# Sharing out small steps of attention and mixing, an early table load, and a new order of the whole program

## The chip, the cores and the metric

The program runs on one core of a Trainium2 chip. The time is device microseconds from one launch, and the value compared is the median of several runs. All work of the core is in one program: TensorE (PE) multiplies, VectorE (DVE), ScalarE (ACT) and GpSimd (POOL) do everything elementwise, and SyncE (SP) issues the DMAs.

## The reference

Attention with a mask by blocks of 64 positions, then a mixer over the joined heads. The inputs q, k, v are 8 batches x 8 heads x 576 positions x 64; the mixer's weights are 512 x 512, 576 x 576 (two) and 512 x 512. All is float32.

```python
scores = q @ k.transpose(0, 1, 3, 2) / sqrt(D)
scores = where(pos[:, None] // 64 >= pos[None, :] // 64, scores, -1e9)
attn = exp(scores - scores.max(-1)); attn = attn / (attn.sum(-1) + 1e-9)
x = (attn @ v), heads joined: [8, 576, 512]
theta = x @ w_theta
zr, zi = x * cos(theta), x * sin(theta)
y = einsum('ts,bsd->btd', w_tok_r, zr) + einsum('ts,bsd->btd', w_tok_i, zi)
u = x + y
out = u + maximum(u @ w_ch, 0)
```

## The kernel before

The eight batches go through two phases that overlap: while batch b is mixed, the attention of batch b + 1 is computed. Heads are taken in pairs (p from 0 to 31, four to a batch; head n = 2p + hh). For accuracy most products are made of two halves: a float32 operand is split into a high and a low part, and three products stand for one. The first twelve pairs use plain float32 scores, the first four pairs plain float32 weights of attention, turned by TensorE.

The program is a list of 2757 parts. A part is a small function with a key; it issues one or a few instructions, nearly always on one engine. PLACES gives each part its place, the list is sorted by it, and the instructions are issued in that order, so that the order in which each engine takes its work is written out by hand. BANKS gives the PSUM bank to each group of products in the order of their starts; a group waits until the former user of its bank has been read. ON gives, letter by letter, the engine of those parts that more than one engine can do (D VectorE, A ScalarE, P GpSimd). RUNNING lists filling products: at a place, so many products of the constant `ones` into a bank that nobody needs (L1113). Waits between engines follow from the data.

The parts that matter here, with the lines that stand in the profile:

- `sab`, `sc`, `sd` (L600, L605, L612): the scores of a pair in three groups. `m` (L638, L630) on VectorE takes the maxima out of PSUM, `e` (L642) on ScalarE the exponentials.
- `tp`, `cp` (L654, L661, L663): for the first four pairs, transposes by TensorE and their copies out of PSUM. For the others `high` and `low` (L327 or L331, L669) split the exponentials into `p`, and a transposing DMA makes `pt`.
- `vz`, `vr`, `vb`, `vm` (L505, L509, L353, L359): the size of a batch's v: two sums over pieces on ScalarE, one addition on VectorE, a diagonal on GpSimd, one product on TensorE. The scale of v follows, then the scaled v (`vf`, or `v1` and `v2`, L586).
- `weighted` (L689): the weighted sums of one head, with the sum of the weights in an extra column.
- `normalise`, steps 0 to 3 (L697 or L699, L701, L706, L709): a small number is added, the reciprocal taken, four or five tiles of 64 columns are multiplied by it out of PSUM into `x_ring` in one instruction on VectorE (step 2), and for the second head of a pair a block of 64 rows more (step 3).
- `again` (L715): a block of 64 rows by 64 columns of `x_ring` is copied to the other 64 partitions, twice for a pair, on GpSimd.
- The mixer: `xh`, `xl` split x (L325 or L331, L775); `theta` (L789) multiplies; `turns` and `rest` (L799, L805) reduce the angle, `size` (L811) takes its absolute value; `sines`, steps 0 to 2 (L823, L825), take cosine and sine, step 0 and 1 of two wide tiles each, step 2 of the last, narrow one; `z`, `zh`, `zl` (L835, L325 to L331, L848) multiply by x and split; `mix` (L858) multiplies by the token weights, `u` (L871) collects; `c` (L891) multiplies by the channel weights, `out` (L897) and `fin` finish, and a DMA stores.

Sine and exponential are not in one table of ScalarE: the build puts a table load ahead of the first activation that needs the other one (ACT_TABLE_LOAD; it carries the line of that activation and stands behind the activation's wait).

Of the kernel before, what the change touches and what calls it, by code (L numbers as in the profile page):

```python
# [32 lines left out]
    3, 2, 15, 19, 21, 62, 162, 197, 4, 5, 22, 30, 34, 65, 177, 191, 27, 26, 52, 61, 64, 92, 246, 255, 43, 40, 74,  # L33
    78, 91, 113, 217, 221, 73, 69, 103, 106, 112, 118, 212, 236, 99, 96, 131, 136, 139, 172, 239, 244, 116, 145,
    154, 165, 167, 219, 227, 146, 182, 226, 234, 242, 252, 429, 578, 178, 174, 198, 229, 249, 256, 361, 449, 82,
    85, 107, 111, 121, 135, 143, 151, 183, 187, 193, 196, 204, 206, 207, 356, 268, 271, 301, 310, 330, 348, 358,
    375, 185, 195, 275, 343, 383, 411, 392, 415, 419, 0, 1, 11, 7, 33, 10, 39, 35, 70, 12, 86, 101, 9, 45, 48, 50,
    53, 55, 57, 60, 63, 284, 499, 287, 130, 179, 77, 152, 324, 81, 125, 345, 328, 157, 370, 377, 173, 192, 233,
    247, 250, 253, 267, 274, 290, 523, 951, 684, 423, 521, 366, 565, 546, 347, 553, 609, 612, 492, 630, 705, 547,
    575, 596, 605, 618, 623, 640, 645, 647, 788, 1284, 903, 686, 528, 716, 771, 790, 712, 844, 899, 894, 753, 993,  # L40
    982, 843, 855, 875, 878, 882, 886, 896, 902, 948, 1073, 1600, 1131, 1022, 1017, 1090, 1104, 1093, 1036, 1192,
    1220, 1205, 1117, 1319, 1306, 1143, 1164, 1208, 1212, 1221, 1226, 1237, 1239, 1245, 1255, 1434, 1574, 1371,
    1367, 1362, 1478, 1443, 1424, 1460, 1564, 1561, 1439, 1671, 1676, 1472, 1507, 1513, 1516, 1532, 1547, 1549,
    1559, 1590, 1680, 2121, 1878, 1739, 1704, 1760, 1835, 1735, 1766, 1846, 1926, 1842, 1742, 1974, 1948, 1818,
    1852, 1868, 1904, 1937, 1947, 1950, 1961, 1964, 1984, 2227, 2165, 2071, 2016, 1997, 2130, 2099, 2102, 2139,
    2234, 2229, 2120, 2329, 2324, 2118, 2156, 2164, 2167, 2204, 2207, 2236, 2270, 2273, 2517, 2546, 2549, 6, 67, 8,
    16, 13, 14, 18, 25, 29, 17, 28, 24, 31, 32, 36, 47, 38, 51, 20, 44, 49, 41, 46, 72, 94, 108, 120, 37, 42, 54,
    59, 93, 117, 119, 124, 266, 122, 126, 23, 76, 58, 66, 56, 68, 75, 84, 88, 80, 79, 87, 83, 104, 98, 97, 102,
    100, 90, 89, 95, 105, 110, 129, 153, 158, 160, 123, 134, 109, 115, 147, 181, 186, 189, 273, 188, 272, 71, 132,
    292, 114, 138, 142, 128, 133, 144, 150, 156, 137, 141, 140, 149, 155, 161, 164, 163, 159, 175, 184, 180, 190,  # L50
    201, 216, 224, 225, 171, 176, 166, 170, 214, 230, 240, 254, 258, 248, 295, 127, 168, 289, 194, 199, 169, 200,
    208, 205, 203, 202, 220, 215, 223, 218, 209, 211, 213, 222, 210, 228, 232, 231, 237, 241, 261, 269, 276, 235,
    245, 238, 243, 264, 283, 285, 291, 298, 288, 300, 148, 303, 362, 251, 282, 302, 259, 270, 297, 294, 320, 277,
    279, 281, 286, 306, 316, 307, 326, 325, 311, 322, 318, 332, 368, 379, 381, 382, 329, 344, 339, 351, 385, 399,
    401, 418, 438, 413, 431, 262, 319, 335, 359, 364, 374, 365, 388, 373, 372, 387, 396, 402, 409, 406, 389, 391,
    390, 400, 404, 417, 427, 426, 433, 476, 488, 489, 490, 425, 443, 442, 450, 498, 513, 514, 535, 539, 522, 534,
# [176 lines left out]
def attention_phase_mixer(  # L233
# [10 lines left out]
    nc = tc.nc  # L244
# [922 lines left out]
```

## Time and profile before

| | |
|---|---|
| median of 3 runs | 663.51 us (662.39 to 667.03) |
| profiled execution, own time | 661.59 us |
| span from first to last instruction | 659.8 us |
| TensorE products, busy | 643.2 us (97%) |
| VectorE, ScalarE, GpSimd busy | 580.5, 466.7, 328.2 us |
| granted clock of TensorE, mean | 0.997 |

The profiled execution is one of many and has its own time; its span is what the profiler saw between the first and the last instruction. A busy TensorE is not one at its peak: products overlap, and their ends are modelled.

### The profile page before, as it was taken

The numbers are of one execution on the slowest core, as the hardware profiler recorded it, in microseconds if no ns is written. First come the engines' busy times: TensorE is split into PE (matmuls) and PEld (weight loads), VectorE is DVE, ScalarE is ACT, GpSimd is POOL, SyncE is SP. The second block draws the span as 40 slices with busy tenths as digits, with TensorE's granted clock in tenths as the row PEclk, the third lists the DMA queues.
The fourth block names the chain that finished last, engine by engine and source line by source line (L and its number), as shares of the span: only waits on it lengthen the run. The fifth ranks groups of instructions, "written<-read, shape, count | busy, mean of one in ns | idle before, by whom it ended". The sixth has DMA issues, their size and how long they took to land.

```text
span 659.8 us, 17344 instructions
## 1 busy us (share of the span) xinstructions
PE 643.2 (97%) x7153; PEld 504.0 (76%) x7153; DVE 580.5 (88%) x900; ACT 466.7 (71%) x719; POOL 328.2 (50%) x345
## 2 busy tenths in 40 slices
PE   8999989999999999999999999999999999999997
PEld 4899767887678767787787868887787867885775
DVE  4899999989999999999998998999879999754724
ACT  4997897775997788665984679678885887516411
POOL 2310357545528737585256466554574346552800
PEclk9999989999999999999999999999999999999999
DMA  8972288999999799699687879899678887740021
GB/s 308 352 254 77 47 205 145 201 221 180 229 199 182 175 190 192 144 202 177 158 201 187 150 177 183 185 210 240 120 175 160 139 192 131 113 114 19 1 90 73
DMA packets 247647, 110.51 MB, mean 167 GB/s; under 512 B 229008, under 2 KB 229008, under 8 KB 247568
## 3 DMA queue, kind: packets, MB, share of 16 engines
q1 hardware_dynamic: 247568, 109.41, 75.3%
q8 instruction: 56, 0.92, 0.6%
q14 instruction: 23, 0.19, 0.1%
HBM read 43.06 MB, written 9.44 MB: 80 GB/s over the span
## 4 chain that ended last, share of the span: by engine, by line
PE 68%; DVE 21%; ACT 5%; issue 4%; DMA 1%; POOL 0%; DVEq 0%; ACTq 0%; POOLq 0%
PE ps L858 25%; PE ps L891 10%; PE ps L689 10%; PE ps L789 10%; PE ps L600 9%; DVE m L638 5%; DVE p L669 3%; DVE v L586 2%; ACT t L642 1%; ACT p L327 1%; PE ps L654 1%; DVE zl L848 1%; PE ps L1113 1%; DVE u L897 1%; DVE wT_l L436 1%
## 5 line engine op out<-in xcount | busy, mean ns | idle before, releaser
L642 ACT ACTIVATE t<-ps,m 128x192 f32<-128x192 f32 (+4 forms) x288 | 140.8, 555 | 58.8 <-DVE m L638 40.2
L858 PE MATMUL ps<-wT_h,zl 128*128 128x288 f16 x540 | 155.0, 287 | 2.5 <-DVE zl L848 2.5
L858 PE MATMUL ps<-wT_h,zh 128*128 128x288 f16 x540 | 155.4, 288 | 0.7 <-ACT t L642 0.7
L858 PE MATMUL ps<-wT_l,zh 128*128 128x288 f16 x540 | 154.9, 287 | 0.0
L638 DVE TENSOR_REDUCE m<-ps 128x2 f32<-128x640 f32 (+3 forms) x128 | 117.4, 946 | 12.0 <-PE ps L605 11.5
L858 PEld LDWEIGHTS <-zh 128*128 128x128 f16 x1080 | 106.1, 98 | 27.8 <-issue 1.1
L689 PE MATMUL ps<-v,pt 128*128 128x65 f16 (+2 forms) x2668 | 113.3, 201 | 3.8 <-DVE x_ring L706 2.5
L669 DVE SCALAR_TENSOR_TENSOR p<-t,p 128x1664 f16<-128x1664 f32 x56 | 111.8, 2002 | 2.6 <-ACT p L327 2.5
L891 PE MATMUL ps<-uhl,wch_h 128*128 128x288 f16 x512 | 95.4, 286 | 1.1 <-DVE u L897 1.0
L689 PEld LDWEIGHTS <-pt 128*128 128x128 f16 x2436 | 81.5, 97 | 8.8 <-issue 5.5
L789 PE MATMUL ps<-wth_h,xt 128*128 128x512 f16 (+1 forms) x384 | 87.3, 345 | 0.3 <-DVE u L871 0.3
L789 PEld LDWEIGHTS <-xt 128*128 128x128 f16 (+1 forms) x576 | 46.4, 102 | 43.7 <-issue 2.4
L327 ACT ACTIVATE p<-t 128x1664 f16<-128x1664 f32 x46 | 73.3, 1599 | 3.7 <-DMA pt<-p 3.4
L891 PE MATMUL ps<-uhl,wch_l 128*128 128x288 f16 x256 | 73.2, 286 | 0.0
L858 PEld LDWEIGHTS <-zl 128*128 128x128 f16 x540 | 53.1, 98 | 16.3 <-DVE zl L848 3.2
L715 POOL COPY x_ring<-x_ring 64x64 f32<-64x64 f32 x64 | 37.9, 592 | 49.8 <-DVE x_ring L709 22.0
L891 PEld LDWEIGHTS <-wch_h 128*128 128x128 f16 x512 | 48.6, 98 | 14.8 <-issue 2.2
L789 PE MATMUL ps<-wth_l,xt 128*128 128x512 f16 (+1 forms) x192 | 57.3, 344 | 0.0
L835 POOL TENSOR_TENSOR aa<-aa,x_ring 128x512 f32<-128x512 f32 (+1 forms) x27 | 34.1, 1265 | 43.0 <-ACT aa L823 32.1
L775 POOL TENSOR_TENSOR xp<-x_ring,xp 128x640 f16<-128x640 f32 x17 | 28.6, 1682 | 34.2 <-ACT xp L325 21.3
L848 POOL TENSOR_TENSOR zl<-aa,zh 128x512 f16<-128x512 f32 (+1 forms) x27 | 33.7, 1252 | 16.4 <-ACT zh L325 12.9
L871 DVE SCALAR_TENSOR_TENSOR u<-ps,gain,u 128x288 f32<-128x288 f32 x64 | 31.2, 507 | 11.9 <-PE ps L858 11.9
(189 smaller groups left out, 1305.0 us busy)
## 6 DMA issues: line engine op xcount, KB each, us to landing
raw_v<-in_v SPq DMA_DIRECT2D x32, 384.0 KB, 4.7
q<-in_qT SPq DMA_DIRECT2D x32, 320.0 KB, 4.0
k<-in_kT SPq DMA_DIRECT2D x32, 320.0 KB, 4.0
out<-u SPq DMA_DIRECT2D x32, 288.0 KB, 3.1
w_raw<-in_w_tok SPq DMA_DIRECT2D x5, 576.0 KB, 4.4
p<-in_w_tok SPq DMA_DIRECT2D x4, 576.0 KB, 5.8
pt<-p SPq DMA_TRANSPOSE x112, 4.5
w_raw<-in_w_theta SPq DMA_DIRECT2D x2, 512.0 KB, 5.1
```

Source lines behind the costliest of these rows:

```text
L327: engine.mul(to, x, scale)
L600: nc.tensor.matmul(s[hh][:, col:col + n], lhsT=qq[rows, i * P:(i + 1) * P], rhs=kk[rows, k0:k0 + n], start=nn == 0 and (j == 0 or c == "ab ...
L638: nc.vector.tensor_reduce(out=m, in_=s, axis=AX.XY if i in (2, 3) else AX.X, op=ALU.max, negate=True)
L642: nc.scalar.activation(out=to, in_=s, func=AF.Exp, scale=1.0, bias=m)
L669: nc.vector.scalar_tensor_tensor(out=self.p[:, 1, :], in0=self.t, scalar=LIFT, in1=self.p[:, 0, :], op0=ALU.mult, op1=ALU.subtract)
L689: nc.tensor.matmul(to, lhsT=pp[:, block, :], rhs=x, start=nn == 0, stop=nn == n - 1)
L715: nc.gpsimd.tensor_copy(out=x[64 - 64 * hh:P - 64 * hh], in_=x[rows])
L789: nc.tensor.matmul(g[rows, 0:cols.stop - cols.start], lhsT=x[:, dt, part, i, rows], rhs=ww[:, dt, cols], start=(n == 0), stop=(n == 11))
L835: engine_of("z", (2 * self.b + hf) * 5 + n).tensor_tensor(out=cd, in0=cd, in1=x, op=ALU.mult)
L848: engine_of("zl", (2 * self.b + hf) * 5 + n).tensor_tensor(out=zl, in0=cv, in1=zh, op=ALU.subtract)
L858: nc.tensor.matmul(g, lhsT=zz[:, kk, cols], rhs=ww[:, kk, ts], start=(n == 0 and kk == k0 and nn == 0), stop=(n == 4 and nn == 2))
L891: nc.tensor.matmul(g[:, 0:HS], lhsT=ww[:, dt, e * P:(e + 1) * P], rhs=uu[:, dt, th * HS:(th + 1) * HS], start=(n == 0), stop=(n == 11))
```

## The change

Four things change, and with them the whole order.

1. Step 2 of `normalise` is done by ScalarE for 19 of the 64 heads, in four or five instructions of 64 columns; step 3 by ScalarE for 17 of 32 pairs; the copies `again` by ScalarE (17), VectorE (23) or GpSimd (24). Three new strings of letters say where. All other strings are new too.
2. A tiny Exp of two columns (`exponentials_next`) is issued at the program's start and behind step 2 of `sines` of each batch. By the new places step 2 is the last of the three steps in batches 1, 2, 3, 5, 6 and 7; in batch 0 the order on ScalarE is `sines` step 2, step 0, step 1 (as before the change), in batch 4 step 2, an `e` of pair 22, step 0, step 1.
3. `ones` is set by VectorE at the start instead of by GpSimd after other constants.
4. RUNNING has 30 filling products in place of 40: 5 before the first scores (3 before), 17 before the first transposes (4 before the rest of the first scores and 23 before the transposes), none before the product `vm` of batch 0 (5), none before the scores of pair 5 (5), 2 and 6 before the weighted sums of heads 8 and 9 (none).

PLACES and BANKS are written anew. At the start the new order has `tp` of all four halves of pair 0 ahead of `vm` of batch 0 (three halves before), then `sab`, `sc`, `sd` of pair 1 (`sd` stood first). VectorE scales the first q (GpSimd did). In batch 0 ScalarE's order around the sines becomes: `high` of head 9, `turns` 4 and 2, `size` 2, `sines` 2 and the tiny Exp, `turns` 3, 1, 0, `size` 1 and 0, `sines` 0 and 1, then `e` of pair 5. The first `mix` takes the bank that `e` of pair 5, head 0, tile 0, leaves; so did the first one before.

```diff
 RUNNING = [
-    (8, 0, 3), (13, 4, 4), (37, 7, 23), (53, 2, 5), (359, 5, 5)
+    (9, 0, 5), (35, 5, 17), (365, 3, 2), (375, 3, 6)
 ]
...
-      "qh": "PPPPPPPDPPAAPAADPAADAPADAAPADDAP",
+      "qh": "DPDAAAPAPDAAPAPPDAAAAAAPPAAPDDAP",
...
-      "n0": "DAADDAADDDDAAADADADDADDADDDADDADDADDDADDDAAADADDADAAAADAAADADADD",
-      "v1": "DDDDPAPDPPPAADPAAAADADPAPPPAADPA",
-      "high": "DDDDDDDDAAAAAAAAAAAADAAADAAAAAADAADADAAADAAAAAADAAAAADAAADAADAAA",
-      "kh": "DDDDDDDDDDDDPAAAPAPAAADPPADAPAAA",
-      "kl": "DDDDDDDDDDDDDPPPDDDPDPDPDDDPPDDP",
+      "n0": "DADAADADDDDADDAAADDDDDADDAAADDDDADDADDDDADDDADDADDDAAADADADDDDAD",
+      "v1": "DDDDPPDAPPDPAAPAADADDPPAAAAAPAAD",
+      "high": "DDDDDDDDDAAAAADAAAAADAAAAAAAADAADAAADAAADAAADAAAAAAADDAAADDADDAA",
+      "kh": "DDDDDDDDDDDDDADPADPPPDADADAPPDAA",
+      "kl": "DDDDDDDDDDDDDPDPPPPPDPPPDPDPPDPP",
...
-      "uh": "AAAAADADAAAAADAA",
-      "fin": "PDAPDDDADDPPPADAADPAPADAAPPADDDDAPDPADDA"}
+      "uh": "DAAADDADAAAAADDA",
+      "fin": "PAADPPAAPPDPAAADPAAAAAAPAADDDDDDDDAAAADA",
+      "n2": "DDDDAADDDDDADDDDDDDDAADDADDAAAADADDADDADDDDDDDDDDDDDDADAADDAAADD",
+      "n3": "ADADDAAADDAADDAADADDADAADDADADAA",
+      "ag": "DADAAAPPDPDAAPAPDDPDADPADDDDPDPPPAPDPPADPAADDDPPAPAADDPPPDAPDPDP"}
...
+    ones = const.tile([P, P], BF16, name="ones")
+    nc.vector.memset(ones, 1.0)
+    spare = const.tile([P, 2], F32, name="spare")
+    nc.vector.memset(spare, 0.0)
+
+    def exponentials_next():
+
+        nc.scalar.activation(out=spare[:, 1:2], in_=spare[:, 0:1], func=AF.Exp)
+
+    exponentials_next()
...
-    ones = const.tile([P, P], BF16, name="ones")
-    nc.gpsimd.memset(ones, 1.0)
...
-                nc.vector.tensor_tensor(out=m.xns[pair.pr][:, 0:n, hh, :], in0=o[:, 0:n, 0:D],
-                                        in1=self.r[:, 0:n].unsqueeze(2).broadcast_to([P, n, D]), op=ALU.mult)
+                to = m.xns[pair.pr][:, 0:n, hh, :]
+                if engine_of("n2", self.n) is nc.scalar:
+                    for i in range(n):
+                        nc.scalar.mul(to[:, i], o[:, i, 0:D], self.r[:, i:i + 1])
+                else:
+                    nc.vector.tensor_tensor(out=to, in0=o[:, 0:n, 0:D], in1=self.r[:, 0:n].unsqueeze(2).broadcast_to([P, n, D]), op=ALU.mult)
             else:
-                nc.vector.tensor_scalar(out=m.xns[pair.pr][0:64, 4, 0, :], in0=o[0:64, 5, 0:D], scalar1=self.r[0:64, 5:6],
-                                        scalar2=None, op0=ALU.mult)
+                times(engine_of("n3", pair.p), m.xns[pair.pr][0:64, 4, 0, :], o[0:64, 5, 0:D], self.r[0:64, 5:6])
...
-        nc.gpsimd.tensor_copy(out=x[64 - 64 * hh:P - 64 * hh], in_=x[rows])
+        to, engine = x[64 - 64 * hh:P - 64 * hh], engine_of("ag", 2 * p + hh)
+        if engine is nc.scalar:
+            engine.copy(out=to, in_=x[rows])
+        else:
+            engine.tensor_copy(out=to, in_=x[rows])
...
+            if n == 2:
+                exponentials_next()
```

## Rows read from the trace of the kernel before

**Rows 1.** The page's busy times: engine, us, share of the span, instructions.

```profile
PE 643.2 (97%) x7153; PEld 504.0 (76%) x7153; DVE 580.5 (88%) x900; ACT 466.7 (71%) x719; POOL 328.2 (50%) x345
```

**Rows 2.** Stretches: sum; busy PE, PEld, DVE, ACT, POOL; PEclk; DMA; GB/s.

```profile
0.00:20.00 20.00, 16.90 (x86) 9.92 (x87) 10.59 (x14) 10.80 (x17) 3.58 (x24) 1.00 0.87 320
...
80.00:100.00 20.00, 18.05 (x173) 11.98 (x172) 19.76 (x34) 19.56 (x30) 9.53 (x12) 0.91 0.82 201
...
220.00:240.00 20.00, 18.99 (x199) 12.19 (x197) 19.62 (x27) 13.51 (x21) 9.93 (x7) 1.00 0.83 186
240.00:260.00 20.00, 18.78 (x243) 15.27 (x242) 20.00 (x30) 17.37 (x24) 13.33 (x10) 1.00 0.95 189
260.00:280.00 20.00, 19.16 (x238) 16.04 (x236) 19.58 (x30) 15.22 (x27) 12.52 (x12) 1.00 0.63 137
...
340.00:360.00 20.00, 18.91 (x238) 15.84 (x237) 17.98 (x29) 8.97 (x13) 9.75 (x13) 1.00 0.78 179
...
380.00:400.00 20.00, 20.00 (x206) 13.17 (x202) 19.89 (x29) 17.24 (x25) 11.46 (x7) 1.00 0.68 162
...
480.00:500.00 20.00, 18.54 (x220) 15.21 (x219) 16.48 (x24) 13.90 (x23) 12.98 (x14) 1.00 0.70 162
```

**Rows 3.** Order of time, 0 to 30 us: start, us, engine, line, operation, tiles.

```profile
8.01 1.28 ACT L416 ACT_TABLE_LOAD   x1 [8.01 <-DMA w_raw<-in_w_theta]
...
11.58 5.14 PE L1113 MATMUL ps<-ones 128*128 128x512 bf16 x23
...
18.52 0.19 ACT L505 ACTIVATION_READ_ACCUMULATOR unused<-raw_v 128x1 f32 x1
...
18.84 1.24 PE L1113 MATMUL ps<-ones 128*128 128x512 bf16 x5
...
19.57 0.14 DVE L509 TENSOR_REDUCE sizes<-sizes 128x1 f32<-128x2 f32 x1
...
20.26 0.22 PE L359 MATMUL ps<-unused,ones 128*128 128x128 bf16 x1 [0.17 <-POOL unused L353]
...
21.27 2.00 PE L600 MATMUL ps<-k,qh 64*128 64x288 f32 x16
```

**Rows 4.** Order of time on ScalarE, 82 to 98 us and 475 to 494.

```profile
84.14 1.02 ACT L823 ACTIVATE aa<-aa,half_pi 64x256 f32<-64x256 f32 x2
...
92.71 1.04 ACT L825 ACTIVATE rr<-rr 128x1024 f32<-128x1024 f32 x1
...
94.27 1.28 ACT L642 ACT_TABLE_LOAD   x1
95.57 2.83 ACT L642 ACTIVATE t<-ps,m 128x320 f32<-128x320 f32 x6
...
483.05 1.28 ACT L642 ACT_TABLE_LOAD   x1 [3.02 <-DVE m L638]
```

**Rows 5.** Order of time on TensorE, 76 to 102 us.

```profile
94.71 2.08 PE L689 MATMUL ps<-v,pt 128*128 128x65 f16 x45 [1.95 <-DVE x_ring L706]
96.58 0.45 PE L858 MATMUL ps<-wT_h,zh 128*128 128x288 f16 x1
```

**Rows 6.** Short stretches behind that wait, columns as in rows 2.

```profile
95.00:97.00 2.00, 2.00 (x43) 1.88 (x40) 2.00 (x5) 1.99 (x5) 1.92 (x3) 0.66 0.28 102
97.00:99.00 2.00, 2.00 (x11) 1.23 (x9) 1.97 (x4) 2.00 (x6) 2.00 (x3) 0.50 0.00 0
```

**Rows 7.** Groups by line: count | busy us, mean ns | idle before, releasers.

```profile
L706 DVE TENSOR_TENSOR x_ring<-ps,r 128x256 f32<-128x256 f32 (+1 forms) x64 | 28.4, 445 | 0.4
...
L709 DVE TENSOR_SCALAR x_ring<-ps,r 64x64 f32<-64x64 f32 x32 | 8.7, 271 | 0.8
...
L642 ACT ACTIVATE t<-ps,m 128x64 f32<-128x64 f32 x32 | 10.2, 319 | 6.6 <-DVE m L630 6.6
...
L715 POOL COPY x_ring<-x_ring 64x64 f32<-64x64 f32 x64 | 37.9, 592 | 49.8 <-DVE x_ring L709 22.0 <-DVE x_ring L706 16.0 <-DVE sizes L509 6.6
```

More of the change, by code (lines that the diff above doesn't have):

```diff
@@ L32 @@
 PLACES = [
[142 rows of a table removed]
[142 rows of a table added]
 ]
 BANKS = [
[12 rows of a table removed]
[12 rows of a table added]
 ]
 RUNNING = [
-    (8, 0, 3), (13, 4, 4), (37, 7, 23), (53, 2, 5), (359, 5, 5)
+    (9, 0, 5), (35, 5, 17), (365, 3, 2), (375, 3, 6)
 ]
-ON = {"w5": "DAADDADAD",
-      "wc": "DDPPPPDDD",
-      "vc": "PDDPDPPPPDPPDPPDDPPDDPPP",
-      "qh": "PPPPPPPDPPAAPAADPAADAPADAAPADDAP",
-      "vf": "PPDPPPPP",
-      "cp": "DDDADAADAADDAAAAAAAAAAAAAAAAAAAA",
-      "n0": "DAADDAADDDDAAADADADDADDADDDADDADDADDDADDDAAADADDADAAAADAAADADADD",
-      "v1": "DDDDPAPDPPPAADPAAAADADPAPPPAADPA",
-      "high": "DDDDDDDDAAAAAAAAAAAADAAADAAAAAADAADADAAADAAAAAADAAAAADAAADAADAAA",
-      "kh": "DDDDDDDDDDDDPAAAPAPAAADPPADAPAAA",
-      "kl": "DDDDDDDDDDDDDPPPDDDPDPDPDDDPPDDP",
-      "xh": "AAAADADADDAAADDDADADDAADDAAADDAAAADDADD",
-      "xl": "DDDDDPPPPDDPDPDPDDDDDDPPDDPPPDPPPPDDDDP",
-      "z": "DPPDDPPDDPPDDDPPPDPDDPPDPPPDPPDDPDDDPPPDPPPDPDPDDPPDDDPPDPDPDDDPPDPPPPPPPDPDDDPD",
-      "zh": "PAADPAPAAAPPDDPAAAAPPDDAAAAPDPPAPADAAPAPAADAAAPAAAADPPAAAAAAPPPADDADAPAAPAAADAAA",
-      "zl": "DPDDDPPPDPPPDDDDPDPDPPDDPDPPPPPPPDDPPPPPDPPPPDPPPDPPPDPPPPPDPDPPDPPPDDPDDDPPDPPP",
-      "xs": "DDPDPPPDPPPDPPDD",
-      "xd": "AAPAAPAADDAAAPAP",
-      "uh": "AAAAADADAAAAADAA",
-      "fin": "PDAPDDDADDPPPADAADPAPADAAPPADDDDAPDPADDA"}
@@ new lines @@
+ON = {"w5": "DDADDADAD",
+      "wc": "PPPDDPPPP",
+      "vc": "PDDPDDDPDPDPPPPPPPPDDPDP",
+      "qh": "DPDAAAPAPDAAPAPPDAAAAAAPPAAPDDAP",
+      "vf": "PPPDPPPP",
+      "cp": "DDDADAADADADAAAAAAAAAAAAAAAAAAAA",
+      "n0": "DADAADADDDDADDAAADDDDDADDAAADDDDADDADDDDADDDADDADDDAAADADADDDDAD",
[3 more added lines that the diff above has]
+      "kl": "DDDDDDDDDDDDDPDPPPPPDPPPDPDPPDPP",
+      "xh": "AAAAAAADADAAADDDAAADDAADDADADDAAAADADAD",
+      "xl": "DDDDDDPPPDDPDPDPPDDDDDPPDPDPPDPPPDDPPPD",
+      "z": "DDDPPPPDPDPDPDDPDDDDPPDPPPPDPPDPDPPDPPDPDPPPPPDPDDDPPDDDPPPPPPPPDPDDPPDDDPPDDDPD",
+      "zh": "PDPAPDPAAAPAPADAPPAPPAAPADDAAPAAPPPAAADDAPAADDPAAAAPPPPAAPDDAPADAADDAAAPAAADDAAA",
+      "zl": "DPPDPPPDPPPPPDPDPPDDDPPPDPPPPPPDDDDPDPPPPPDDPPPPDPPDPPDPDPDPPDPPDPDDDPPPPDDDDPPP",
+      "xs": "DDPDPDPPPDPDPPDD",
+      "xd": "ADAAAADAADAAAPAA",
+      "uh": "DAAADDADAAAAADDA",
[3 more added lines that the diff above has]
+      "ag": "DADAAAPPDPDAAPAPDDPDADPADDDDPDPPPAPDPPADPAADDDPPAPAADDPPPDAPDPDP"}
```

308 rows, old and new, of tables (BANKS, PLACES) are left out of this document.

## Prediction

> **What bounds the kernel now.** I read the busy shares first, then the stretches of 20 us, then the order of time at the two places where TensorE stands still longest. TensorE is busy for 643.2 of 659.8 us [rows 1], so 16.6 us of idle time is all that the records leave, and VectorE has 88% behind it. In the stretches [rows 2] the reader is to look for those in which PE's sum is short of 20.00, and at who is full there. In the first stretch PE is short by 3.10 us, and 35 of its products are fillers (40 in all, L1113): they multiply `ones` while nothing else is ready. From 80 to 100 it is short by 1.95, and VectorE (19.76) and ScalarE (19.56) are both full. From 220 to 280 it is short by 1.01, 1.22 and 0.84, with VectorE at 19.6 to 20.0; at 340 and 480 by 1.09 and 1.46. Elsewhere the sums are 20.00, as at 380. So this is a kernel in which TensorE's work sets the time, and a change gains only what it takes off the start, off VectorE's queue where VectorE holds TensorE back, and off the waits near 95 and 490.
>
> How records and time stand to each other: the span is 659.8 us, the profiled execution took 661.59, and the median of the three timed runs is 663.51, which is 1.92 above it. I sum against 661.59 and add 1.92 at the end.
>
> **The start.** The first product that depends on the batch's scale of v is L359, at 20.26 [rows 3]. It waits for this: ScalarE ends the second sum of v (L505) at 18.71; VectorE adds them (L509) only at 19.57, because two copies out of PSUM (L663) stand ahead in its queue; then come GpSimd's diagonal and L359. The scores of pair 1 (L600) follow at 21.27, behind five transposes and a small product, 1.01 us in all. In the new order the four halves of the transposes come ahead of L359, the small product (0.17 of work) comes after the scores, and both copies ahead of L509 start earlier, since ScalarE no longer begins its first work with the table load of 1.28 us at 8.01 [rows 3]. By the order of the new list and the durations of these rows VectorE is through with the copies by about 18.6, so L509 follows the second sum at once, L359 is at about 19.4, and the scores of pair 1 at 19.5: 1.77 earlier, 1.6 after the small product is paid. Bounds: nothing, if VectorE is as late as now; 3.3 us, if every filler stood for real waiting, for behind the first scores there were 32 of them in this stretch and there are 17 now (15 at 0.22, from 5.14 us for 23). The first fillers (three, now five) end before q has landed and cost nothing; `ones` set by VectorE and the first q scaled by VectorE instead of GpSimd are worth about 0.1, since k lands at the same time.
>
> There is a price. The five fillers between the transposes and L359 (18.84) are gone, and by the same working TensorE has nothing from about 17.4 to 19.4. The one such hole of the trace is the wait of 1.95 us that ends at 94.71 [rows 5]; after it the granted clock was 0.66 and then 0.50, which is 1.2 of 2.4 GHz [rows 6], and 2 x 0.34 + 2 x 0.50 = 1.7 us were lost. I give that an even chance at the start, so I count the start at -1.6 + 0.8 = **-0.8** (ends -3.3 and +1.7).
>
> **ScalarE's table.** Now an Exp behind the sines begins with a table load of 1.28 us that stands behind the wait for the maxima: at 483.05 it begins after a wait of 3.02 us on `m`, so the exponentials come 1.28 later than they could [rows 4]. The change runs one tiny Exp at the start and one behind the third step of sines of each batch, so that the load falls into the wait. That is a gain where the third step is the last. By the new places it is not in batches 0 and 4: there the third step comes first, then the tiny Exp with its load, then the other sines with a second load of their own, then the exponentials with a third. 16 loads become 21: two more in batch 0, two in batch 4, one behind the last sines. In batch 0 this falls where ScalarE is full. Now it goes from the first sine at 84.14 to the last near 93.7, loads from 94.27 to 95.55, and does six exponentials from 95.57 [rows 4]; the first mixing product follows at 96.58. With the new order, from the first sine to the end of the first of the wide steps (91.76 now) come 1.28 + 0.2 for load and tiny Exp, 1.28 for the second load, and 0.6 for one more L799 that is now done earlier, less 0.25 of waiting: 3.1 us more. Against it the stretch before is shorter: one L327 of p (1.6) and one of v (0.9) have gone to VectorE and GpSimd, and the first sine waits for VectorE's L805; I put it 1.3 earlier. So the wide sines end at 93.6 and 95.6, the load at 96.9, the second exponential at 97.7; the first mixing product takes the PSUM bank which that one leaves, and starts at 97.8 in place of 96.58: **+1.2**. Ends: nothing (ScalarE so much earlier that the loads hide), and 2 x 1.28 + 1.7 = 4.3 for both loads and one more fall of the clock. The two loads of batch 4 fall near 400, where PE is full and ScalarE has 17.24 of 20 [rows 2]: hidden by mixing and channel products, nothing (+2.6 if that cover fails). The load behind the last sines has nothing left to delay.
>
> By the Trainium skill ("ScalarE: Activation LUTs", Table sets: the hidden batching unit) all functions of one table set are to be done before switching; this speaks against the new order in these two batches. The same page (What ACT_TABLE_LOAD costs) prices a switch at 2.66 us, drain included. Here the load took 1.28, and the next activation began 0.02 later (94.27 to 95.57), so the trace shows no drain; by the page's price the term would be +4.0 and the sum 662.5.
>
> **The steps shared out.** 19 of the 64 normalising steps L706 leave VectorE (0.445 each [rows 7], 8.5 us), 17 of the 32 L709 (0.271, 4.6 us). Of the 64 copies L715, 24 stay on GpSimd (0.592 each), 17 go to ScalarE, 23 to VectorE; their cost there is not in the trace. The nearest rows are L709 on VectorE (64 rows by 64 columns, 0.271, from PSUM) and the exponential of 64 columns on ScalarE (0.319); I take 0.2 on VectorE (4.6 us in all; 3 to 6). A step L706 on ScalarE becomes four or five instructions of 64 columns: 4.5 x 0.2 to 0.32, so 0.9 to 1.4 for the 0.445 that it replaces. The other letters of the table change too: VectorE gets five more of `kh`, four of `high`, three of `uh`, and loses five of `kl` and four of `fin`; by the rows of their lines this puts some 7 us back. VectorE's total thus stays as it is (-1.6 of 580, an estimate), GpSimd loses about 28, ScalarE gains about 24 and the loads.
>
> So where the relief falls decides. Of the nineteen, eight are in heads 24 to 39 and three of the L709 too: counted with the other letters, VectorE has about 6 us less in these two batches and slightly more (0.5 to 2.3) in batches 0, 2, 6 and 7. These heads run from about 225 to 360, where VectorE holds PE back. The idle time of PE there, with the hole at 480 that a load ahead shortens by its 1.28, is 1.01 + 1.22 + 0.84 + 1.09 + 1.46 = 5.6 us [rows 2]. I take three quarters, **-4.2**: VectorE is relieved by more than is idle, but ScalarE, which feeds it, has more to do. Ends: nothing, and -7.3 with the 1.7 that is left of the 16.6 us beside the start, 80 to 100, these five, and some 4.2 behind the last product. What is late next is ScalarE's exponentials, in whose queue the new pieces now stand ahead of the next pair's; TensorE's scores wait for the banks that they leave.
>
> The eight fillers before the last two weighted products of batch 0 stand in a wait; for the five that go (1.1 us) nothing is counted (+0.7 if the three more push work back). TensorE's other products are the same, and in the last 80 us it has no hole before or after.
>
> **Sum:** -0.8 + 1.2 - 4.2 = -3.8: 657.8 beside the profiled 661.59, so **659.7** beside the median.
>
> **Rivals.**
> - VectorE stays the bound: its sum does not change, and it runs 19.6 to 20.0 in every stretch with holes. For it: the new list has VectorE some 2 us more burdened up to about 220. Against: the relief lies just behind. The -4.2 falls away: 663.9.
> - Everything is recovered: the loads of batch 0 hide behind what ScalarE sheds, the clock holds at the start, and the holes close. For it: over the span ScalarE is at 71% [rows 1], so it can run ahead. Start -3.3 to -1.6, holes -7.3: 652.9 to 654.6.
> - Slower: ScalarE becomes the bound in batch 0, at 80 to 100. It is at 19.56 of 20 [rows 2]; if it cannot begin its sines earlier, both loads are on the path (2.6), the hole before the first mixing product passes 2 us, and the clock falls as at 95 (1.7); the same in batch 4 for 2.6. That is 6.9, and it decides from the point where it exceeds the 5.0 of the gains: 665.4.
>
> **How the numbers follow.** Chances: my forecast 0.45, all recovered 0.28, VectorE still the bound 0.17, slower 0.10. The range reaches from the far end of the second rival, 653, past the third and the slower one to 666; above lies the slower one joined by a fall of the clock at the start. About 1% (6.6 us) is what a measurement of this kernel can tell from no change. Faster by more than that, under 656.9: the second rival and a sixth of my own case, 0.35. Slower than 670.1: 0.05. Else 0.60.
>
> **What would show it.** Start: L600 of pair 1 near 19.5, and the granted clock 0.5 or 1.0 behind it. Table: 21 loads; four near 82 to 97; the first L858 near 97.8. Relief: PE's sums at 220 to 280 nearer to 20.00 and VectorE's below 19.5. I am wrong if PE's holes move instead of closing, with ScalarE named as what ends them; or if the first mixing product comes well before 96, which would mean that the two further loads were hidden.

## The result, and the profile after

The changed kernel takes 672.54 us (median of 4 runs, 672.05 to 673.23) beside 663.87 for the kernel before: a ratio of 1.0125 (1.0087 to 1.0163). It is slower by a little over 1%, and outside the range that was given. The ratios here and below are estimates from the runs, with their 95% intervals, and not quotients of the medians. The experiments were timed on other chips, each group beside the kernel before (medians 661.53 to 662.61), so that their ratios compare better than their times. The profiled execution took 672.83 us, with a span of 671.0, which is 11.2 more than before.

The page's busy times [rows 1] come first:

```profile
PE 644.2 (96%) x7143; PEld 504.5 (75%) x7143; DVE 587.0 (87%) x900; ACT 495.9 (74%) x845; POOL 309.9 (46%) x301
```

TensorE's idle time went from 16.6 to 26.8 us. VectorE, which was to be left where it was, has 6.5 us more.

The stretches of 20 us, columns as in [rows 2]:

```profile
0.00:20.00 20.00, 15.69 (x79) 9.77 (x79) 11.97 (x17) 11.49 (x19) 3.40 (x22) 1.00 0.93 339
80.00:100.00 20.00, 17.96 (x179) 11.08 (x178) 19.00 (x30) 19.58 (x30) 7.79 (x9) 1.00 0.65 151
100.00:120.00 20.00, 17.89 (x181) 13.94 (x181) 19.34 (x23) 15.85 (x23) 13.11 (x11) 1.00 0.90 201
220.00:240.00 20.00, 20.00 (x216) 13.97 (x214) 19.94 (x25) 15.10 (x29) 11.50 (x7) 1.00 1.09 220
240.00:260.00 20.00, 16.66 (x168) 13.34 (x167) 18.05 (x26) 15.13 (x21) 11.22 (x10) 0.83 0.60 142
260.00:280.00 20.00, 18.27 (x261) 15.46 (x260) 17.08 (x25) 15.30 (x30) 11.38 (x8) 1.00 0.90 141
320.00:340.00 20.00, 18.48 (x219) 13.38 (x214) 18.32 (x30) 16.77 (x26) 9.06 (x11) 1.00 0.95 194
340.00:360.00 20.00, 20.00 (x233) 16.66 (x230) 19.37 (x31) 13.62 (x26) 8.90 (x9) 1.00 0.58 133
460.00:480.00 20.00, 18.48 (x212) 11.90 (x209) 18.73 (x25) 14.10 (x22) 8.90 (x7) 1.00 0.81 165
480.00:500.00 20.00, 20.00 (x245) 16.63 (x242) 19.01 (x29) 18.95 (x29) 19.21 (x15) 1.00 0.74 159
```

The holes at 220, 340 and 480 are closed, as was hoped. Those at 240 and 260 have grown (3.34 and 1.73 are missing), and the largest new ones stand at 100, 320 and 460 (2.11, 1.52, 1.52). In most of these stretches VectorE is not full (100 is nearest, with 19.34): at 260 it works 17.08 of 20 while TensorE lacks 1.73. Where both are idle in the same stretch, the amount of VectorE's work is not what holds TensorE back. Holes of 0.3 us and more between 30 and 660 us, counted from TensorE's rows, are 10 with 8.3 us in the kernel before and 16 with 17.0 us now.

The largest is at 251. Order of time on VectorE, GpSimd and TensorE there (POOL is GpSimd):

```profile
248.28 2.85 DVE L680 SCALAR_TENSOR_TENSOR p<-t,p 128x1664 f16<-128x1664 f32 x1
...
250.09 2.15 POOL L855 TENSOR_TENSOR aa<-aa,x_ring 128x512 f32<-128x512 f32 x1 [0.71 <-ACT aa L841]
...
251.14 1.36 DVE L733 COPY x_ring<-x_ring 64x64 f32<-64x64 f32 x2
252.53 1.19 DVE L917 SCALAR_TENSOR_TENSOR u<-ps,u 128x288 f32<-128x288 f32 x3
...
253.77 0.60 PE L611 MATMUL ps<-kh,qh 64*128 64x288 f32 x1 [2.56 <-DVE u L917]
```

And the short stretches behind it, columns as above:

```profile
252.00:254.00 2.00, 0.23 (x2) 0.23 (x4) 1.96 (x6) 0.00 (x0) 0.25 (x1) 0.76 0.74 170
254.00:256.00 2.00, 2.00 (x20) 2.00 (x21) 1.18 (x4) 1.38 (x3) 1.20 (x1) 0.50 0.32 126
256.00:258.00 2.00, 2.00 (x20) 2.00 (x19) 1.00 (x1) 1.91 (x5) 2.00 (x3) 0.50 0.00 0
258.00:260.00 2.00, 2.00 (x14) 1.35 (x11) 2.00 (x4) 1.08 (x2) 2.00 (x4) 0.54 0.00 0
```

Read the first from below. The scores (L611) wait for the PSUM bank that the channel output (L917) leaves. L917 stands in VectorE's queue behind two of the moved copies (L733), and these take 1.36 us: GpSimd's product (L855) runs from 250.09 to 252.24, and the first copy, begun at 251.14, ends 0.05 later. The low half of p ahead of them (L680, 2.85 us) runs beside another product of GpSimd; most of the 56 such instructions take 1.88. The granted clock of the four stretches is 0.76, 0.50, 0.50 and 0.54, that is 1.2 of 2.4 GHz for 6.8 us. That is 2 x (0.24 + 0.50 + 0.50 + 0.46) = 3.4 us of clock, but in the first stretch TensorE still stands still for most of it; counted from 253.77, where it starts again, about 3.0 us are lost. The kernel before has one such fall in mid-run, for 1.7 [rows 6].

This is one execution. The four timed runs of the changed kernel have mean granted clocks of 0.994 (the profiled one), 0.997, 0.999 and 0.995, and took 672.83, 672.25, 672.05 and 673.23 us: the one with 0.999 lost at most 1 us of clock in its whole span and is only 0.8 shorter than the profiled one. So the 3.0 us are in the trace, but it is not shown that they come off the time when the clock holds.

All copies of that line on the two engines (count; shortest/median/longest in ns):

```profile
L733 POOL COPY x_ring<-x_ring x24: 231/233/788, 74.4 to 596.3; 64x64 f32<-64x64 f32 x24
L733 DVE COPY x_ring<-x_ring x23: 183/192/1155, 57.3 to 595.8; 64x64 f32<-64x64 f32 x23
```

The groups by line that answer to [rows 7]:

```profile
L722 DVE TENSOR_TENSOR x_ring<-ps,r 128x256 f32<-128x256 f32 (+1 forms) x45 | 20.1, 446 | 2.3 <-ACT x_ring L338 1.9
L733 DVE COPY x_ring<-x_ring 64x64 f32<-64x64 f32 x23 | 9.6, 420 | 0.6
L342 DVE TENSOR_SCALAR x_ring<-ps,r 64x64 f32<-64x64 f32 x15 | 4.0, 269 | 0.2
L720 ACT ACTIVATE x_ring<-ps,r 128x64 f32<-128x64 f32 x86 | 19.6, 319 | 9.9 <-DVE r L712 9.4 <-DVE x_ring L342 0.6
```

A copy has a median of 192 ns and a mean of 420. All nine that took over 0.3 us began while an instruction of GpSimd ran, and ended 0.04 to 0.05 us after it.

The start, order of time (answers to [rows 3]); then ScalarE's loads in batch 0 and the first mixing product (to [rows 4, 5]):

```profile
18.68 0.19 ACT L516 ACTIVATION_READ_ACCUMULATOR unused<-raw_v 128x1 f32 x1
...
18.90 0.15 DVE L520 TENSOR_REDUCE sizes<-sizes 128x1 f32<-128x2 f32 x1 [0.20 <-ACT unused L516]
18.97 0.81 DVE L674 TENSOR_SCALAR pt<-ps 128x640 f32<-128x640 f32 x1
...
19.84 0.23 PE L370 MATMUL ps<-unused,ones 128*128 128x128 bf16 x1 [1.38 <-DVE pt L674]
...
20.00 2.00 PE L611 MATMUL ps<-k,qh 64*128 64x288 f32 x16
...
81.65 1.28 ACT L841 ACT_TABLE_LOAD   x1
...
84.86 1.28 ACT L284 ACT_TABLE_LOAD   x1
...
90.14 1.28 ACT L841 ACT_TABLE_LOAD   x1
...
95.54 1.28 ACT L653 ACT_TABLE_LOAD   x1
...
97.73 0.28 PE L878 MATMUL ps<-wT_h,zh 128*128 128x288 f16 x1 [1.11 <-ACT t L653]
```

To place the loss I read the traces at equal work: every product counts as the usual distance to the next one of its form in the kernel before, the fillers count as nothing, and two traces are compared where the sums are equal. How many us a kernel is behind the one before (four of the experiments beside it):

```
us in    changed  old, new   new, old   copies as   old order,
before   kernel   from 222   from 224   a reduce    mended
               (e10)      (e9)       (e12)       (e14)
 30.7     -0.2     -0.1       -0.3        0.2        -0.7
100.9     -0.1      0.3       -0.8        0.1        -0.5
114.0      2.3      0.3        3.5        1.2         0.0
243.1      2.1     -0.2        5.8        1.8         0.9
258.2      6.7      3.3        5.4        2.6        -0.3
271.1      5.6      2.2        5.4        1.5         1.6
332.3     10.3      5.7        5.7        5.7         2.0
354.9      7.8      3.2        5.7        3.2         2.0
427.6      8.7      3.9        5.7        3.9         2.0
477.2     13.9      8.6        6.2        9.2         2.0
502.0     10.4      5.2        6.2        5.7         0.2
516.4     11.5      6.4        6.2        6.8         2.4
627.3     11.3      7.0        6.4        6.2         2.1
```

Steps up that come back a little later are products in another order, or holes of the kernel before. At 114 the changed kernel is 2.3 behind and e12 1.2: there too a copy of VectorE waits, 1.15 us from 104.63. By 243 most of that difference is gone.

### The profile page after: what moved, and what is told of

The parts are those of the page before. It is cut to its first block, busy times and chain, and to the rows that moved or that the text cites. A ratio compares the mean times of both kernels' runs of the same rounds, so it can differ in the third digit from the quotient of the medians.

```text
span 671.0 us, 17398 instructions
## 1 busy us (share of the span) xinstructions
PE 644.2 (96%) x7143; PEld 504.5 (75%) x7143; DVE 587.0 (87%) x900; ACT 495.9 (74%) x845; POOL 309.9 (46%) x301
## 4 chain that ended last, share of the span: by engine, by line
PE 57%; DVE 27%; ACT 7%; issue 4%; DMA 4%; POOL 0%; SPq 0%; DVEq 0%; ACTq 0%
PE ps L878 19%; PE ps L911 12%; PE ps L700 10%; PE ps L611 7%; PE ps L807 7%; DVE p L680 6%; DVE m L649 6%; ACT t L653 3%; DVE v L597 2%; DVE ql L576 1%; DVE rr L823 1%; DVE u L891 1%; DMA raw_v<-in_v 1%; DVE zl L868 1%; DMA pt<-p 1%
## 5 line engine op out<-in xcount | busy, mean ns | idle before, releaser
L653 ACT ACTIVATE t<-ps,m 128x320 f32<-128x320 f32 (+4 forms) x288 | 142.0, 555 | 59.9 <-DVE m L649 32.6
L680 DVE SCALAR_TENSOR_TENSOR p<-t,p 128x1664 f16<-128x1664 f32 x56 | 113.5, 2028 | 2.4 <-ACT p L338 2.2
L338 ACT ACTIVATE p<-t 128x1664 f16<-128x1664 f32 x42 | 66.5, 1591 | 0.8 <-DMA pt<-p 0.3
L611 PE MATMUL ps<-kh,qh 64*128 64x288 f32 (+2 forms) x240 | 41.6, 321 | 5.6 <-DVE u L917 2.6
L581 POOL TENSOR_TENSOR kl<-k,kh 128x640 fp32r<-128x640 f32 x14 | 32.5, 2321 | 27.7 <-ACT kh L560 13.5
L855 POOL TENSOR_TENSOR aa<-aa,x_ring 128x512 f32<-128x512 f32 (+1 forms) x24 | 32.4, 1351 | 25.8 <-ACT aa L841 18.3
L611 PE MATMUL ps<-k,qh 64*128 64x224 f32 (+3 forms) x288 | 39.8, 413 | 3.0 <-DMA k<-in_kT 1.4
```

The costliest lines, as they stand in the source:

```text
L338: engine.mul(to, x, scale)
L581: engine_of("kl", self.p).tensor_tensor(out=self.kl, in0=self.k, in1=self.kh.bitcast(F32), op=ALU.subtract)
L611: nc.tensor.matmul(s[hh][:, col:col + n], lhsT=qq[rows, i * P:(i + 1) * P], rhs=kk[rows, k0:k0 + n], start=nn == 0 and (j == 0 or c == "ab ...
L653: nc.scalar.activation(out=to, in_=s, func=AF.Exp, scale=1.0, bias=m)
L680: nc.vector.scalar_tensor_tensor(out=self.p[:, 1, :], in0=self.t, scalar=LIFT, in1=self.p[:, 0, :], op0=ALU.mult, op1=ALU.subtract)
L855: engine_of("z", (2 * self.b + hf) * 5 + n).tensor_tensor(out=cd, in0=cd, in1=x, op=ALU.mult)
```

## The experiments

Two theories at first: the pieces on ScalarE (the normalising steps and copies moved there) and the further table loads delay the exponentials; or the new order itself waits in more places.

**Parts undone in the new order, and the small edits in the old one.**

```diff
e1  -            if n == 2:
    -                exponentials_next()
e2  -      "n2": "DDDDAADDDDD...", "n3": "ADADDAAADD...", "ag": "DADAAAPPDP..."
    +      "n2": "D" * 64, "n3": "D" * 32, "ag": "P" * 64
e3   PLACES, BANKS, RUNNING and twenty strings of the kernel before, all else of the change
e4   the twenty older strings of the kernel before, all else of the change
```

> The changed kernel without the tiny Exp behind the third step of sines of each batch (the one at the start stays): 16 or 17 table loads instead of 21. If the extra loads on ScalarE are what costs the time (four loads in batch 0 and two more in batch 4, at 1.28 us, with the holes that they open): 664 to 668. If the order of the work costs it: 670 to 674, no more than 2 us from the 672.5 of the changed kernel.

> The changed kernel with the three new choices of engine undone: all 64 normalising steps and 32 steps of 64 rows on VectorE, all 64 copies on GpSimd, in the order of the changed kernel. If the pieces on ScalarE cost the time, because they stand ahead of the exponentials for which TensorE waits: 662 to 667. If the order costs it: 670 to 676; above 674 if VectorE, with some 13 us more, is then the bound.

> The kernel before with its order, banks, fillers and old engine choices, and only the small edits: tiny Exps, ones set by VectorE, and the new choices of engine for normalising steps and copies. If the new order costs the time: 658 to 666, like the kernel before or a little faster, since VectorE is relieved. If the pieces on ScalarE or the tiny Exps cost it: 669 to 674.

> The changed kernel, its order and its new choices kept, but the older twenty groups of work on the engines that did them before. If the other letters, which put some 7 us back on VectorE, cost the time: 663 to 668. If the order itself (which work stands behind which) costs it, whoever does it: 670 to 678, since the order was not made for these engines.

Measured: e1 674.09, 1.0183 (1.0160 to 1.0206); e2 671.90, 1.0156 (1.0115 to 1.0197); e3 700.34, 1.0576 (1.0538 to 1.0614); e4 715.57, 1.0806 (1.0784 to 1.0828). Neither the loads nor the pieces are the cause by themselves: both come out with the order. (e1 still makes 18 loads: it takes away two in batch 0 and one at the end, and in batch 4 four remain.) In e3 and e4 both theories missed, the second by 34 and 38 us: an order and the engines that it was made with belong together. e2 is worth a look at its waits (TensorE; us in all, times, longest):

```profile
PE ps L700 <- ACT t L653: 3.1, 1, 3.1
```

With no copy on VectorE the hole at 251 is down to 0.77, but at 320 the weighted sums now wait 3.1 us for exponentials, and the clock falls there instead. Its runs spread from 669.83 to 675.36; the profiled one took 673.83.

**One part alone in the old order.** Order, banks, fillers and old strings of before; e7 has the new strings for the normalising steps, e8 those for the copies (both with the Exp and `ones` at the start).

```diff
e7  +      "n2" and "n3" of the change, "ag": "P" * 64
e8  +      "ag" of the change, "n2": "D" * 64, "n3": "D" * 32
```

> The order, banks and engines of the kernel before; of the change only the normalising steps that go to ScalarE (19 of 64 and 17 of 32), ones set by VectorE and the tiny Exp at the start. Together with the next kernel it splits the 38 us that the small edits cost in the old order. If instructions that wait on TensorE's sums stop ScalarE's queue, where the exponentials stand: 680 to 700. If they cost only their own time on an engine with room: 662 to 666.

> The same, but only the 64 copies of 64 rows shared out (24 GpSimd, 23 VectorE, 17 ScalarE) and no normalising step moved. If copies stand in VectorE's and ScalarE's queues behind steps that are not done, or in VectorE's behind an instruction of GpSimd: 670 to 690. If they cost only their own time: 662 to 666.

Measured: 674.10, 1.0157 (1.0122 to 1.0192), and 675.65, 1.0193 (1.0171 to 1.0215). Taking 13 us of work off VectorE makes the old order 12 us slower; the copies make it 13.6 slower. For e8 that is what the queues were expected to do; e7 lies between its two theories.

**Over from one order to the other.** At part 987 the two lists have all but two parts in common behind them, so a kernel can go over there; each part keeps its list's engine and bank.

```diff
e5  places 0 to 986 of the new list, the rest in the order of the old one
e6  places 0 to 986 of the old list, the rest in the order of the new one
e9, e10  the same without
    -            if n == 2:
    -                exponentials_next()
```

> The first 987 of the 2757 pieces of work in the order of the changed kernel (up to about 224 us), the others in the order, on the banks and on the engines of the kernel before. If the time is lost in places of the new order, each by itself, this keeps the 3 us that the new order has lost up to there and none of the 8 that it loses later: 664 to 667. If the loss is carried along whatever comes behind: 670 or more.

> The reverse: up to 222 us the kernel before, from there the order, banks and engines of the changed kernel. If the time is lost in places: some 8 us over the kernel before, 669 to 672. If the beginning sets up the later holes: 661 to 665.

Measured: 674.88, 1.0185 (1.0162 to 1.0207), and 671.21, 1.0133 (1.0107 to 1.0159). These two don't tell the theories apart: in the old order the third step of sines is the last one only in batch 2, and the tiny Exps left there made 28 and 23 table loads. Without them:

> As the earlier kernel that goes over from the new order to the old at 224 us, but without the tiny Exps behind the third step of sines: in the old order that step is mostly not the last, so there they cost 10 table loads in five batches. If the new order loses its time in places of its own: the 2 to 3 us of its first 224 us and no more, 663 to 666. If the old order, begun 2 to 3 us later, falls out of step: 668 or more.

> The reverse at 222 us, also without the tiny Exps. If the new order loses its time in places of its own: the some 9 us of its later part, 669 to 672. If those extra loads were 4 of the 9 us of the earlier kernel of this kind and the new order needs its own beginning to lose the rest: 664 to 667.

Measured: 666.73, 1.0059 (1.0033 to 1.0085), and 670.00, 1.0094 (1.0067 to 1.0121). The first is a little over what was expected, the second within it. The two losses, 4.1 and 7.4, make 11.5, beside 8.7 between the medians of the changed kernel and the one before, and 11.2 between their spans. The table shows the shape: from 243 on the old order keeps its 5.7 us to the end and adds 0.7, and the new order, begun in step, makes nearly the same steps at the same places as the changed kernel. So most of the time is lost in places of the new list. Not all of e9's 5.7 is: the changed kernel is only 2.1 behind at 243. The profiled execution of e9 is 1.3 above its median, has a fall of the clock at 112 that the changed kernel's has not, and behind the seam a hole of 1.67 at 241 that stands in neither kernel.

**The table loads.** `last_sines` names the step that is last in the list.

```diff
e11 (kernel before)
    +    last_sines = (1, 1, 2, 0, 1, 1, 1, 1)
    ...
    +    exponentials_next()
    ...
    +            if n == last_sines[self.b]:
    +                exponentials_next()
e16 (e12, below)
    -            if n == 2:
    +    last_sines = (1, 2, 2, 2, 1, 2, 2, 2)
    ...
    +            if n == last_sines[self.b]:
```

> The kernel before, and nothing of the change but the table loads ahead: one tiny Exp at the start and one behind that step of sines which is the last of its batch in the order. If a load ahead is worth its 1.28 us where ScalarE waits: 655 to 661. If any shift in the queues of this tight order costs something: 662 to 668.

> The changed kernel with the copies as a reduce, and the tiny Exp behind that step of sines which is the last of its batch in the new order: 17 loads in place of 21. If the loads of batch 0 are on TensorE's path: the loss near 100 to 115 goes, 665.5 to 667. If they are hidden: 667 to 669.

Measured: e11 662.03, 0.9985 (0.9971 to 0.9999), so 0.6 us gained between the medians, and between 0.1 and 1.9 by the interval: the second theory, just. e16 668.95, 1.0090 (1.0066 to 1.0115), nothing beside e12. It made 19 loads, not the 17 expected: batch 0 is down to two, batch 4 still has four, since exponentials of a pair stand between its sines. In e11 the load moved up from 483.05 to 479.59, and the hole that it was to shorten is still there (1.46 before); it waits for VectorE's `zl`, not for the exponentials:

```profile
479.59 1.28 ACT L280 ACT_TABLE_LOAD   x1
...
499.74 0.30 PE L869 MATMUL ps<-wT_h,zl 128*128 128x288 f16 x1 [1.58 <-DVE zl L859]
```

**The copies.** The new suspect is the wait of VectorE's copies for GpSimd. The Trainium skill ("SBUF — State Buffer", Who interferes with whom) says that VectorE and GpSimd share one pair of ports, which an instruction holds to its end; that a `copy` can run in a mode that needs it; and that `tensor_reduce` on trn2 never does. The rows above agree with the first two: the copies that waited ended 0.04 to 0.05 us after GpSimd's instruction. The third is the experiment: the same copy as a maximum over one element, in the new order (e12) and in e8 (e17).

```diff
+        elif engine is nc.vector:
+            engine.tensor_reduce(out=to, in_=x[rows].unsqueeze(2), op=ALU.max, axis=AX.X)
         else:
             engine.tensor_copy(out=to, in_=x[rows])
```

> The changed kernel, with the 23 copies of 64 rows on VectorE written as a maximum over one element, which is another instruction with the same result. If a copy waits for GpSimd's instruction to end because both use one way into the memory, and this one does not: 0.2 to 0.3 us for each in place of 0.19 to 1.16, the hole at 251 shrinks from 2.6 to about 1.5, and the time is 668 to 671. If the hole has another cause or the gain is given back behind it: 671 to 674.

> The kernel before with only the 64 copies shared out, as once already (675.7), but VectorE's 23 as a maximum over one element. If waiting for GpSimd is most of what these copies cost: 664 to 669. If it is their place in VectorE's and ScalarE's queues: 671 to 676.

Measured: e12 668.02, 1.0077 (1.0052 to 1.0102), its slowest run (670.76) below the fastest of the changed kernel; e17 675.80, 1.0215 (1.0197 to 1.0232), no gain. In e12, VectorE's copies; then the order of time at the old place, and the stretch behind it:

```profile
L733 DVE TENSOR_REDUCE x_ring<-x_ring x23: 208/214/216, 57.5 to 590.5; 64x64 f32<-64x64 f32 x23
```

```profile
250.80 0.44 DVE L733 TENSOR_REDUCE x_ring<-x_ring 64x64 f32<-64x64 f32 x2
...
251.27 1.19 DVE L919 SCALAR_TENSOR_TENSOR u<-ps,u 128x288 f32<-128x288 f32 x3
...
252.51 0.40 PE L611 MATMUL ps<-kh,qh 64*128 64x288 f32 x1 [1.64 <-DVE u L919]
```

```profile
254.00:256.00 2.00, 2.00 (x28) 1.75 (x26) 1.66 (x3) 1.90 (x5) 2.00 (x2) 1.00 0.43 157
```

No copy waits any more (208 to 216 ns, with GpSimd at work beside 14 of the 23). The hole goes from 2.56 to 1.64, and the clock stays at 1.00: 0.92 + 3.0 = 3.9 us by the rows of the two executions, 4.1 in the table at 258 and 271, 3.2 by the ratios and 4.5 between the medians (1.3 of which the kernel before differs by). In the table the gain stays to the end. How it divides between the hole and the clock is not shown beyond these two executions: the runs with a mean clock of 0.999, 672.05 of the changed kernel and 667.49 and 667.76 of e12, lie as far apart. In e17 the copies take 214 ns as well, and the time is where its second theory had it. The old order has other waits: the weighted sums of head 24 wait 3.15 us, and VectorE's queue ahead of them reads, with GpSimd's beside it:

```profile
227.93 2.75 DVE L342 TENSOR_SCALAR v<-raw_v,sizes 128x768 f16<-128x768 f32 x1
230.59 2.68 DVE L902 SCALAR_TENSOR_TENSOR uhl<-u,size_ch,uhl 128x1152 f16<-128x1152 f32 x1
...
227.15 3.10 POOL L883 TENSOR_TENSOR u<-xt 128x1152 f32<-128x1152 f16 x1
230.22 1.84 POOL L581 TENSOR_TENSOR kl<-k,kh 128x640 fp32r<-128x640 f32 x1
...
233.89 2.30 PE L700 MATMUL ps<-v,pt 128*128 128x65 f16 x39 [3.15 <-DVE u L891]
```

In the kernel before the same two VectorE instructions take 0.61 and 1.40 us, and another one ahead of them met GpSimd's sum (which ran from 220.77 to 223.15):

```profile
220.81 3.15 DVE L586 SCALAR_TENSOR_TENSOR v<-raw_v,sizes,v 128x768 f16<-128x768 f32 x1
223.88 0.61 DVE L331 TENSOR_SCALAR v<-raw_v,sizes 128x768 f16<-128x768 f32 x1
224.41 1.40 DVE L882 SCALAR_TENSOR_TENSOR uhl<-u,size_ch,uhl 128x1152 f16<-128x1152 f32 x1
```

Moved by a few us, the same list collides elsewhere.

**What is left.** e15 is e12 with three GpSimd instructions on VectorE, e18 with only the last of them; e14 is e11 with six pieces moved in the old order, at its four largest holes.

```diff
e15 -  xs of batch 3, second half, and z of batch 2, half 0, piece 3:  "P"     + "D"
e15, e18
    -  xs of batch 5, first half:  "P"                                         + "D"
e14 +  normalise 0, 1, 2 of head 8 ahead of m.5.1;  zl.5.0.3 ahead of qh of pair 29
    +  out.1.3.1 ahead of m.15.3;  kl of pair 21 behind zl.3.0.4
```

> The changed kernel with the copies as a reduce, and three long GpSimd instructions moved to VectorE: two sums of halves of x (pair of tiles 1 of batch 3, 0 of batch 5) and one product z of batch 2. If what is left of the loss comes from VectorE's instructions waiting for GpSimd's: the holes at 320 and 461 close by some 1.4 each, 664 to 666. If VectorE's own 3.6 us more outweigh that: 668 to 671.

> The changed kernel with the copies as a reduce and one sum of halves of x (batch 5, first pair of tiles) moved from GpSimd to VectorE, so that the low part of p at 457 us no longer waits for it. If the gain of that place stays to the end: 665.5 to 667. If it is given back: 667.5 to 669.

> The kernel before with the table loads ahead (behind the true last step of sines) and six pieces moved in its order, at its four largest holes: the three normalising steps of head 8 ahead of the maxima m.5.1, a low half of z (batch 5) ahead of two long VectorE pieces, one channel output ahead of a maximum, and GpSimd's low half of k (pair 21) behind the VectorE piece that it blocks. The holes are 1.95, 1.46, 1.09 and 1.02 us. If a hole that is mended stays closed: 656 to 660. If each pushes its wait to the next place: 661 to 665.

Measured: e15 667.68, 1.0073 (1.0046 to 1.0099); e18 667.18, 1.0088 (1.0066 to 1.0110); e14 663.71, 1.0026 (1.0006 to 1.0047). e15 and e18 lie between their two theories; e14 is where the second had it. First e12 around 457, where GpSimd's sum stands beside the low half of p, then e15:

```profile
456.05 2.96 POOL L885 TENSOR_TENSOR u<-xt 128x1152 f32<-128x1152 f16 x1
...
456.69 4.07 DVE L680 SCALAR_TENSOR_TENSOR p<-t,p 128x1664 f16<-128x1664 f32 x1
...
461.72 0.59 PE L809 MATMUL ps<-wth_h,xt 128*128 128x512 f16 x2 [1.37 <-ACT t L653]
```

```profile
457.13 1.88 DVE L680 SCALAR_TENSOR_TENSOR p<-t,p 128x1664 f16<-128x1664 f32 x1
...
461.23 0.59 PE L809 MATMUL ps<-wth_h,xt 128*128 128x512 f16 x2 [0.34 <-ACT t L653]
```

The low half needs 1.88 us and took 4.07. With the sum on VectorE the hole there closes from 1.37 to 0.34; the hole at 320, where I expected the same, stays at 1.37, and with the piece of z that VectorE now does those at 250 and 274 grow (1.85 from 1.64, 1.32 from 0.87), and behind the first the granted clock is 0.5 again for 3.4 us. e18 moves the one sum alone: the hole at 457 is 0.54, most others stay. The ratios don't show a gain in either. In e14 the wait at 93 went from 1.95 to 0.68 and a new one stands right behind it:

```profile
93.74 1.62 PE L692 MATMUL ps<-v,pt 128*128 128x65 f16 x45 [0.68 <-DVE x_ring L709]
...
96.86 0.28 PE L863 MATMUL ps<-wT_h,zh 128*128 128x288 f16 x1 [1.50 <-ACT t L645]
```

The holes at 255 and 497 close too (-1.2 and -1.8 in the table) and 1.9 and 2.2 us come back within 15 us; the one at 349 stays (1.09, now 1.10). No version is clearly faster than the kernel before; e11 comes nearest.

## Why the prediction was wrong, step by step

- **Start, -0.8:** -0.2 at equal work. The addition follows the second sum at once, as said (18.68, 18.90), and the clock stays at 1.00. That is this execution: in e2's, with the same hole of 1.38 before L370, it is 0.50 for 3.4 us from 21.8. But L370 is at 19.84 (19.4 forecast): it waits for one more copy out of PSUM, which VectorE does behind the addition and which I had not counted. The scores come 1.27 earlier instead of 1.77.
- **Table loads, +1.2:** the loads stand where they were said to (21; four from 81.65 to 95.54), and the first mixing product is at 97.73 (97.8 forecast). As a cost it was nothing: e1 without the further loads of batch 0 is no faster, nor is e16. The changed kernel is even with the one before at 101; the 2.3 us come behind it, at 108 to 112. The price of a switch that the Trainium skill gives ("ScalarE: Activation LUTs", What ACT_TABLE_LOAD costs) is not what these rows show: each of the 21 loads takes 1.28, and ScalarE's next activation begins 0.01 later. Batch 4's loads (400.4 to 416.7) cost nothing, as said: TensorE's sums at 380 and 400 are 20.00. No run took them away.
- **VectorE's relief, -4.2: the step that failed.** At equal work, over heads 24 to 39, 5.7 us were lost (2.1 behind at 243, 7.8 at 355) where 4.2 were to be won, and what follows cost another 3.5. Two things in it were wrong. First, its size: VectorE's total rose by 6.5 instead of falling by 1.6. The normalising steps took off what was said (8.3 and 4.7), but the copies cost 9.6, not 4.6, outside my 3 to 6, and by what is left the other letters put 9.9 back, not 7. I took 0.2 from a row with one operand in PSUM (L709), which GpSimd did not draw out: its 32 instructions took 246 to 277 ns, 11 of them wholly beside GpSimd's work. The warning stood in [rows 7]: GpSimd's copies had a mean of 592 ns; the shortest of them took 231, the longest 3550. Second, its bounds: I let the step end at "nothing", so I held that relief can't hurt. A copy in VectorE's queue delays what stands behind it, and at 251 its wait of 1.0 us made a hole of 1.64 (as in e12) one of 2.56, with half clock behind it. I had priced such a fall at the start and at batch 0's loads [rows 5, 6], and not here. Two readings under the term were wrong too. The sums elsewhere are not all 20.00: in the stretches from 20, 160, 180, 200 and 560 they run from 19.26 to 19.83, 1.9 us in all, which the sum had only in its far end, as the 1.7 that is left. And the hole at 480 was no wait for a table load: it waits for VectorE's `zl`, and the load moved ahead left it (1.58 in e11).
- **ScalarE gains about 24, GpSimd loses about 28:** 29.2, the further loads among it, and 18.3. That ScalarE's pieces delay exponentials is seen in single holes, but e2 shows that undoing them gives nothing back.
- **Fillers, 0:** no run tried them alone.
- **The rivals:** none was right. VectorE did not stay the bound, since it has idle time in most stretches with new holes, though in the largest hole it is busy; the slower case put the loss on batch 0's loads, which e1 and e16 rule out. My sign of error came true, "PE's holes move instead of closing", but ScalarE, which was to be named, ends only five of the 16 (6.5 us), and VectorE ten, the largest among them (9.7).

Shown is: most of the loss lies in places of the new list (e9, e10); the copies' waits are 3 to 4 us of it (e12), in the profiled executions through one hole and the clock behind it. The other 6.2 us of e12's span are, by size alone, its holes: 15 with 14.3 us beside 10 with 8.3. That a VectorE instruction drawn out by GpSimd makes the hole is shown for one of these (e15, e18); that this is the cause of them all is not shown. Open is also why the old order fits so well; that mending it brings nothing says only that it has no cheap hole left.

## What to carry to other kernels

Where four engines take their work in a fixed order and two are nine tenths full, moving an instruction is a change to the queue that it joins: ask who stands behind it there, and let the range reach below nothing. A mean far above the median in a group of equal instructions was here a wait inside the instruction; find what runs beside it before you move it to the engine on the other side of that wait. A hole in TensorE's work can have a stretch of half clock behind it, which in the profiled execution more than doubled the largest; look at the clocks of several runs before you put a price on it.

## What was not expected of the hardware

A copy of 64 x 64 in float32 on VectorE took 183 to 192 ns where it did not wait and up to 1155 beside GpSimd; a maximum over one element did the same work in 208 to 216 throughout. Written that way, it was a copy that did not wait.

The same hole can be followed by a fall of the clock or not. Behind the 1.95 us at 93 of the old order the granted clock was 0.5 for 3.4 us in the kernel before, and 1.00 in e11. And a fall in the records need not be seen in the time: of the 58 runs of the kernel before that were timed beside the experiments, the 18 with a mean clock of 1.0 have a median of 661.97 us and the 31 with 0.996 or 0.997 one of 662.16, though 2.0 to 2.6 us of clock lie between them; the six with 0.993 to 0.995 have 665.07.
